# A gated linear-attention block and an MLP on one core: nine of twelve down products by Strassen's scheme

## The chip, the cores and the metric

The kernel runs on one core of one Trainium2 chip. The metric is device time in microseconds, from the start of the program to its end. Beside it one execution is recorded by the hardware profiler, and its page, its groups of instructions, its waits and its instructions in order of time are what this document reads. The engines are TensorE (PE in the profile, with its weight loads as PEld), VectorE (DVE), ScalarE (ACT), GpSimd (POOL) and SyncE (SP, which here only issues transfers). On-chip memory is SBUF; TensorE's results land in PSUM, which here is four pairs of banks.

## The reference

Two blocks follow one another. The first is a recurrence over 768 steps for 4 batches and 8 heads of 40 channels; the second is an MLP over the 3072 tokens that it yields, with 320 inputs, 2048 hidden units and 320 outputs.

```
for t in range(S):                                  # S = 768, state is 40x40 per batch and head
    y[:, :, t] = einsum('bhd,bhde->bhe', r_t, state)
    Sa = einsum('bhde,bhe->bhd', state, a_t)
    state = state * w_t - einsum('bhd,bhe->bhde', Sa, b_t) + einsum('bhd,bhe->bhde', v_t, k_t)
x = y.transpose(0, 2, 1, 3).reshape(3072, 320)
h = x @ w_in                                        # [3072, 2048]
g = h * (1.0 / (1.0 + exp(-1.702 * h)))
return g @ w_out                                    # [3072, 320]
```

All data are float32.

## The kernel before

The 768 steps are cut into twelve chunks of 64. A chunk has two units, each with two of the four batches, so there are 24 units `i = 2 * c + p`. For a unit, `decay` builds products of the decays, `prep` scales a, b and k by them and forms the score matrices, `inverse` inverts a triangular matrix in five levels, and `solve` reads the state, solves, and yields y and the next state. The level loop is a chain over engines: TensorE multiplies into `ps_level`, ScalarE or VectorE copies W out (line 751), VectorE forms E (line 753) and transposes it (line 702), and one of three engines spreads it into EX (lines 704 to 710), which the next level's product reads.

At its end a unit scales y into `x` (line 953) and writes it to DRAM (`part_with`, line 963); `get_back` (line 967) reads it back in the layout that the MLP wants, as `xT`. Both are issued on SP's queue. After a chunk's second unit `mlp(c)` follows for its 256 tokens:

- `up(q, m, k)`, line 978: the hidden layer, in four quarters q; eight matmuls of 256 columns in each of ten steps of a quarter.
- `gelu(q)`, line 987: ScalarE takes a quarter out of PSUM into a tile `g`, four of which exist.
- `down(p)`, line 992: the output of one half of the tokens (batches 2p and 2p + 1), in eight `part(m)` of 16 matmuls. The tokens are the stationary side (64x64), and 320 columns of `w_out_sb` stream past. One bank pair holds the sum over all of the hidden units, its two banks one half of the rows each. ScalarE or VectorE copies one bank to `ob` (line 1012), VectorE adds the other (line 1014), SP stores (line 1011).

A matmul of float32 appears as two instructions in the profile, and `mm` (line 299) is the line of them all. Four matmuls of 64x64 occupy the four quadrants of TensorE's array at once; the text calls four such instructions a pass.

The order of all work is written out by hand. `Plan.add` (line 65) records each piece as a task with the engines that could run it, its reads and writes; `listed` (line 89) reads the string `ORDER`, in which each entry names a task, its engine (p TensorE, a ScalarE, d VectorE, g GpSimd, s SyncE) and, where it uses PSUM, the bank pair. So an entry like `97g` puts task 97 on GpSimd at that place of its queue. The tasks of the MLP fill TensorE between the steps of the units' chains. The weights arrive as 64-bit numbers and are turned to float32 in the first stage (`weight`, line 431), with `extra` as one of the places for the raw numbers.

Of the kernel before, what the change touches and what calls it, by code (L numbers as in the profile page):

```python
# [58 lines left out]
class Plan:  # L59
# [29 lines left out]
    def listed(self, text):  # L89

        assert len(text.split()) == len(self.tasks)
        table, out, done = "exp", [], set()
        for one in text.split():
            e = next(e for e in ENGINES if ENGINES[e] in one)
            n, bank = one.split(ENGINES[e])
            t = self.tasks[int(n)]
            assert e in t.engines and t.after <= done and (e == "SP" or (t.pair is None) == (not bank))
            t.engine, t.bank = e, int(bank or 0)
            if e == "ACT" and t.table:
                t.load, table = t.table != table, t.table  # L100
            done.add(t)
            out.append(t)
        return out
# [4 lines left out]
0s 8s 26s 5s 7s 9s 3a 6s 87p0 88p1 24s 89a1 1s 2s 12s 102a 95d 100p2 90a0 93d 158a 101d2 98p3 96g 10s 94d 17s 97g 16s 99d3  # L108
103p1 4a 11s 132p0 104a1 105d1 142p2 143p3 133a0 106d 130p1 14s 144a3 13s 107p0 15s 18s 151g 108a0 109d0 51s 131a1 110p3 27s
149g 150d 111a3 112d3 159p0 156p1 145a2 161d0 160a0 152g 113p3 345s 92a 162d 25s 153d 114a3 163p2 42s 115d3 34s 19a 274s 264p0  # L110
165d2 265p3 164a2 22d 266a3 166p2 20d 273s 21d 33s 43s 167a2 154p3 168d2 23g 35s 28a 157d1 116p2 155d3 169p1 117a2 118d2 267a0
279d 63s 280g 119p3 277s 171d1 36s 44s 123a3 120d3 343s 125d3 121a 278g 124d3 29d 287a 126p2 170a1 288p0 127a2 30d 172p1 479s
122a3 31d 289a0 128p2 54s 173a1 45s 129d2 32g 62s 174d1 134p3 37a 290d0 175p2 344s 135d3 180a2 146s 178a2 275s 176d2 136p1
179a2 38d 181a2 39d 177a 282g 276s 291d 91s 138a1 182p0 188p3 281d 183a0 186p2 139d 137a1 283p0 187a2 184p1 189a3 40d 140s
292p2 46a 60s 284d0 41g 285p3 185d1 148a 286d3 190p0 293a2 294d2 334p1 335p3 357a 191d0 141s 268g 147s 336a3 315d 192p2 47d
337a1 348d 316p0 194a2 346s 295p3 349d 61s 317a0 195g 347s 358p1 296a3 297d3 360d1 318a0 298p3 271a 361d 319p0 338g 300d3 196s
193a2 320a0 355p2 385d 270s 48d 299a3 362p0 356d2 351g 301p3 363a0 364d0 350g 386p2 197s 302d3 365p0 387a2 269s 352g 359a1
303d3 388a2 323p1 367d0 366a0 321p3 49d 324a1 304p2 322a3 478s 325d1 50g 353p0 309a2 470p3 354d0 209p1 307a2 210p1 310a2 305d2
211p1 308a2 272d 198p0 341a 199p0 72s 212p1 70s 64a 200p0 340s 368p2 52s 342d 339s 69s 201p0 369a2 202p0 370d2 203p0 471a
213p1 65d 214p1 389p2 66d 472a3 483g 204p0 390a2 560s 371p3 67d 306a 53s 215p1 71s 482s 216p1 372a3 217p1 476a 220p2 373d3 68g  # L120
218p1 221p2 477d 219a1 205p0 222p2 206p0 223p2 224p2 78s 559s 207p0 55a 311p3 225p2 79s 312d3 80s 226p2 208a0 58d 313p1 374p3
314d1 227p2 56d 379a3 228p2 229p2 57d 326p0 230a2 59g 393p1 327d0 378a3 391p2 394a1 375d3 231p0 558s 392d2 376a 232p0 233p0
395d1 81s 73a 234p0 480s 381p2 235p0 474s 328p1 475s 382a2 74d 377a3 485d 380a3 236p0 75d 481s 492a 242p2 486d 243p2 82a 76d
484d 77g 383p3 237p0 384d3 244p2 329d1 330d1 488p3 473d 238p0 531d 245p2 487g 246p2 489d3 85d 532p1 708s 239p0 533a1 396p3
331d 534a1 240p0 247p2 397d3 332s 241a0 562s 535p1 83d 490p3 536a1 84d 398p0 706s 572a 491d3 86g 550p1 253p3 399d0 551a 555s
400d0 561s 333s 254p3 401d 255p3 552a1 564d 493p0 402s 556a 567g 570p1 554s 494d0 248p2 705s 563d 566g 249p2 495d0 498d 256p3
571d1 565g 403s 250a2 496a0 251d2 696p1 497g 557d 539p0 252s 537p2 257p3 538a2 704s 540d0 701s 258p3 553d 611d 697a 499d 573p2
259p3 576a2 574d2 784s 710d 700s 260p3 787s 541d0 575d2 404p0 578d 261a3 577g 405p0 579d 698a1 568p2 711g 500p1 406p0 569d2
501a1 407p0 262d3 580p2 702a 502d1 263s 408p0 582d2 409p0 503d 410p0 583d 504a 612p3 411p0 584g 613d3 412p0 614d3 413p0 505p1
709d 414a0 426p3 506d1 427p3 428p3 507d1 429p3 699d 581d2 430p3 615p1 703d 431p3 616a1 785s 585p0 432p3 508d 586a0 433p3 587d0  # L130
434p3 509a 588d 435p3 589d 448p2 436a3 510p1 590p0 511a1 449p2 592d0 591a0 512d1 415p3 513d 416p3 593d 514a 417p3 594g 418p3
515p0 419p3 516a0 517d0 595p1 518d 420p3 596a1 597d1 421p3 598d 422p3 519a 599d 423p3 424p3 520p0 425a3 437p1 521d0 438p1
523d0 522g 439p1 524d0 440p1 525d0 441p1 442p1 526d0 527p3 718p0 528a3 443p1 719d0 929s 444p1 720d0 529p3 445p1 721d0 446p1
530d3 600p0 723d 447a1 542p3 722d 724g 603d0 605a0 619p1 604d0 543d3 450p2 620a1 606d0 544p3 621d1 601d0 602d 617p1 707s 546d3
451p2 618a1 783s 712d 547g 713d 607p0 725p1 608a0 452p2 609p0 453p2 548s 610d0 932s 454p2 727d1 726d1 622p0 728d 545d3 729a
775p1 455p2 623d0 780s 776a 549s 756d 730p3 624p0 456d2 457d2 731d3 458s 459p2 777a1 778g 732d3 786s 788g 781a 779s 626d0
460p2 625d0 627g 733d 795p1 835d 734a 461p2 735p3 791g 462p2 628s 736a3 796d1 737d3 716p0 792g 738d 463p2 782d 739g 1011s
920p1 757p3 925s 464p2 717d0 758a3 629s 759a3 790d 465p2 740p0 789d 466p2 741a0 742d0 921a 797p3 467d2 760p0 1008s 468d2 800a3
923d 652p2 469s 761d0 922a1 653p2 926a 930s 798d3 714p1 799d3 654p2 924s 802d 801g 655p2 934d 803a 656p2 836p0 657p2 715d1
658p2 659p2 837d0 762p3 838d0 927d 660p2 763a3 661p2 764p1 662a2 743d 630p0 744d 928s 631p0 632p0 765d1 804p3 766d1 633p0  # L140
805a3 806d3 634p0 807d 635p0 808a 745p2 636p0 748d2 637p0 749d2 839p1 933g 750d2 638p0 840a1 1009s 751d2 639p0 809p3 746d2
935g 640a0 641p1 810d3 642p1 793p2 747a 811d3 674p0 812d 794d2 813a 752p3 643p1 753a3 814p2 644p1 815a2 816d2 754p3 645p1
755d3 646p1 817d 647p1 818a 767p2 841p3 768d2 648p1 842a3 649p1 819p2 650p1 820a2 821d2 769p3 822d 651a1 823d 675p0 771d3 931s
770d3 772g 824p2 936d 676p0 827a2 828a2 942p1 829a2 677p0 1153s 830a2 937d 945a1 773s 663p3 825d2 664p3 943d1 1156s 826a 665p3
944d1 999p2 947d 946g 666p3 1000a 1004s 980d 940p1 948g 667p3 941d1 668p3 774s 669p3 670p3 831p1 671p3 1001a2 1002d 1003s
832d1 672p3 1005a 1013d 678p0 673a3 1006d 833p2 843p1 679p0 834d2 1007s 844d1 938p2 845d1 680p0 939d2 846p3 681p0 847d3 949p1
1012g 682d0 848p2 950a1 683d0 1014d 684s 685p3 849d2 1015g 1010s 850d2 1021p0 1016g 951d1 686p3 1024a0 1232s 851d 1235s 981p2
687p3 982a2 952d 852s 1022d0 983a2 953g 1144p1 1023d0 688p3 1026d 1145a 1149s 1025d 1027g 984p2 1059d 689p3 1154s 954p0 853s
985a2 1147g 690p3 1158d 1148s 955a0 956d0 986p2 1146a1 957d 1150a 691p3 958d 987a2 1151d 988p0 692p3 989a0 1152s 990d0 959p1
693a3 865p2 960a1 694d3 866p2 961d1 867p2 695s 962d 868p2 963d 1028p0 869p2 1029a0 1030d0 870p2 1031d 1157g 871p2 1159d 1032a  # L150
1060p3 872p2 873p2 1061a3 874p2 1062d3 1033p1 875a2 854p0 1035d1 855p0 1036d 856p0 1037d 1063p3 857p0 1064d3 1034a1 858p0
964p2 859p0 965a2 966d2 1038p1 967d 860p0 1039a1 1040d1 861p0 1041d 1017p3 968a 1042g 862p0 1018d3 863p0 969p2 864a0 876p1
970d2 877p1 972d2 971g 1043p3 973d2 878p1 1044a3 974d2 879p1 975d2 880p1 881p1 1045d3 1019p0 1046d 976p2 1047a 882p1 1020d0
1233s 883p1 977a2 1166p3 884p1 1169a3 1167d3 1377s 978p0 885p1 1168d3 898p2 1171d 1170g 886a1 979d0 887p3 1172a 1048p0 991p1
1051a0 888p3 1052a0 992d1 889p3 1053a0 890p3 1054a0 891p3 1049d0 993p1 1050a 1067p0 994d1 1160g 1155s 892p3 1161d 1068a0 893p3
894p3 1069d0 1380s 895p3 1204d 1065p0 995d1 896p3 996d 1066a0 1231s 1055p1 899p2 897a3 1056d1 997s 1173p0 1223p3 900p2 1174a0
# [92 lines left out]
def rwkv7_gelu_quick(ctx: ExitStack, tc: tile.TileContext, time_d, v_d, w_d, wc_d, ak_d, b_d, rv_d, w_in, w_out, out):  # L249
    nc = tc.nc  # L250
    H, D, S = 8, 40, out.shape[0] // 4
    DM = H * D
    C = 64
    MID = C // 2
    NU = time_d.shape[0]
    PIECE = w_in.shape[2]
    NF = w_in.shape[0] * PIECE // DM
# [717 lines left out]
    def mlp(c):  # L975
# [47 lines left out]
        for p in BITS:  # L1023
            down(p)
# [8 lines left out]
    for i in range(NU):  # L1033
# [10 lines left out]
        if i % 2:  # L1044
            mlp(i // 2)
# [84 lines left out]
```

## Time and profile before

| | |
|---|---|
| median of 3 runs | 680.31 us (679.8 to 680.98) |
| profiled execution | 682.79 us, span 681.1 us |
| VectorE, ScalarE, GpSimd busy | 65%, 49%, 26% |
| mean granted TensorE clock | 0.990 of full speed |
| HBM traffic over the span | 98 GB/s |
| `ps_up` matmuls, 3840 of 256 columns | 254.4 us busy |
| `ps_down` matmuls, 3072 of 320 columns | 240.3 us busy |

A busy time is the union of the group's instructions, with pipelined and modelled ends, so the groups of TensorE overlap. The chain of waits gives `ps_up` 30.7% and `ps_down` 29.7% of the span, without overlap. The page's lines for one group name the line, engine and operation, out<-in with shapes and count, then busy time and the mean in ns, then the idle time of the engine just before, and what ended it.

### The profile page before, as it was taken

To read this page: it belongs to the slowest core of one execution; us is meant where nothing else is said; L and a number is where in the kernel's file an instruction comes from. 1 tells how busy PE (TensorE), PEld (TensorE's weight loads), DVE (VectorE), ACT (ScalarE), POOL (GpSimd) and SP (SyncE) were. 2 spreads that over 40 slices of the span, in tenths; PEclk is the share of its full clock that TensorE was granted. 3 is DMA by queue.
4 is the path that set the end of the run, shared out by engine and by line. 5 is a ranking of instruction groups with operands and counts; after the bars stand their busy time and mean duration, and the time that the engine had idled before them with its cause. 6 is when DMAs were issued, how large, how long until landed. Compare 5 with 4: busy or idle time off the path is not lost.

```text
span 681.1 us, 42181 instructions
## 1 busy us (share of the span) xinstructions
PE 652.0 (96%) x19488; PEld 572.4 (84%) x19488; DVE 445.5 (65%) x906; ACT 330.7 (49%) x688; POOL 176.7 (26%) x204
## 2 busy tenths in 40 slices
PE   5777999999999999999999999999999999999997
PEld 5667888997987788888888898899899799889996
DVE  4687877777867668767776587868556766675001
ACT  4675845544564654664545445455454354252110
POOL 5443444225123123123123211321412421300000
PEclk9788999999999999999999999999999999999999
DMA  7874755205314314432404413513502312200100
GB/s 235 275 244 148 228 158 173 89 14 155 108 50 139 103 45 125 124 108 67 121 23 131 140 34 107 154 33 106 149 29 71 121 51 58 58 13 23 51 12 21
DMA packets 35312, 69.73 MB, mean 102 GB/s; under 512 B 5440, under 2 KB 14656, under 8 KB 35136
## 3 DMA queue, kind: packets, MB, share of 16 engines
q1 hardware_dynamic: 35136, 67.03, 32.8%
q8 instruction: 153, 2.51, 1.6%
q14 instruction: 23, 0.19, 0.1%
HBM read 59.15 MB, written 7.86 MB: 98 GB/s over the span
## 4 chain that ended last, share of the span: by engine, by line
PE 91%; DMA 4%; ACT 1%; DVE 1%; issue 1%; SPq 0%; ACTq 0%; DVEq 0%
PE ps_up L300 31%; PE ps_down L300 30%; PE ps_level L300 9%; PE ps_y L300 5%; PE ps_B L300 4%; PE ps_X L300 2%; PE ps_N L300 2%; PE ps_rz L300 2%; PE ps_RV L300 2%; PE ps_A L300 1%; DMA ak<-in_ak 1%; PE ps_zT L300 1%; PE ps_Q L300 1%; DMA time<-in_time 1%; PE ps_T L300 1%
## 5 line engine op out<-in xcount | busy, mean ns | idle before, releaser
L300 PE MATMUL ps_up<-xT_all,w_sb 64*64 64x256 f32 x3840 | 254.4, 377 | 2.0 <-DMA xT_all<-x_dram 1.1
L300 PE MATMUL ps_down<-w_sb,g 64*64 64x320 f32 x3072 | 240.3, 430 | 1.1 <-issue 0.9
L300 PEld LDWEIGHTS ps_up<-xT_all,w_sb 64*64 64x64 f32 x3840 | 172.9, 133 | 17.7 <-issue 2.5
L300 PEld LDWEIGHTS ps_down<-w_sb,g 64*64 64x64 f32 x3072 | 143.3, 133 | 31.4 <-issue 1.6
L988 ACT ACTIVATE g<-ps_up 128x1024 f32<-128x1024 f32 x48 | 49.1, 1024 | 44.7 <-PE ps_up L300 44.3
L709 POOL TENSOR_TENSOR EX<-ES,quads 128x512 f32<-128x512 f32 x29 | 38.3, 1323 | 115.5 <-DVE ES L702 83.1
L751 ACT COPY W<-ps_level 128x512 f32<-128x512 f32 x56 | 32.7, 585 | 69.1 <-PE ps_level L300 67.4
L300 PEld LDWEIGHTS ps_level<-W,EX 64*64 64x64 f32 x2560 | 59.2, 134 | 5.8 <-DVE T L830 0.2
L300 PE MATMUL ps_level<-W,EX 64*64 64x64 f32 (+1 forms) x2560 | 56.2, 217 | 0.0
L753 DVE TENSOR_TENSOR E<-two,ps_level 128x256 f32<-128x256 f32 x80 | 33.1, 415 | 34.7 <-ACT W L751 30.7
L707 ACT ACTIVATE EX<-ES,quads 128x256 f32<-128x256 f32 x80 | 36.3, 501 | 30.4 <-DVE ES L702 29.9
L619 POOL TENSOR_TENSOR ak<-ak,FT 128x512 f32<-128x512 f32 x16 | 22.0, 1378 | 76.2 <-DMA ak<-in_ak 54.4
L300 PE MATMUL ps_level<-PT,EX 64*64 64x64 f32 (+2 forms) x1280 | 34.9, 244 | 5.7 <-DVE EX L723 4.8
L300 PEld LDWEIGHTS ps_level<-PT,EX 64*64 64x64 f32 x1280 | 32.6, 145 | 8.9 <-DVE EX L723 5.7
L702 DVE STREAM_TRANSPOSE ES<-E 128x256 f32<-128x256 f32 x80 | 35.2, 442 | 4.7 <-DVE E L753 0.5
L300 PE MATMUL ps_y<-M,bh 64*64 64x104 f32 (+1 forms) x768 | 34.8, 247 | 1.3 <-DVE M L907 0.8
L300 PE MATMUL ps_y<-RV,kh 64*64 64x104 f32 (+1 forms) x768 | 34.9, 247 | 0.3 <-DVE EX L723 0.3
L891 ACT COPY B<-ps_B 128x416 f32<-128x416 f32 (+1 forms) x34 | 16.5, 492 | 33.5 <-PE ps_B L300 33.2
L300 PEld LDWEIGHTS ps_y<-RV,kh 64*64 64x64 f32 x768 | 28.9, 133 | 2.0 <-DVE M L907 0.5
L907 DVE TENSOR_TENSOR M<-ps_X,later 128x832 f32<-128x832 f32 (+1 forms) x24 | 23.8, 993 | 9.8 <-PE ps_X L300 9.5
L627 POOL TENSOR_TENSOR kh<-time,G 128x320 f32<-128x320 f32 x18 | 16.2, 902 | 48.4 <-PE ps_y L300 34.4
L300 PEld LDWEIGHTS ps_y<-M,bh 64*64 64x64 f32 x768 | 27.0, 133 | 1.9 <-DVE M L907 1.2
(131 smaller groups left out, 1097.2 us busy)
## 6 DMA issues: line engine op xcount, KB each, us to landing
ak<-in_ak SPq DMA_DIRECT2D x48, 160.0 KB
rv<-in_rv SPq DMA_DIRECT2D x48, 160.0 KB
time<-in_time SPq DMA_DIRECT2D x24, 320.0 KB
xT_all<-x_dram SPq DMA_DIRECT2D x48, 160.0 KB
wc<-in_wc SPq DMA_DIRECT2D x20, 264.0 KB
logw<-in_w SPq DMA_DIRECT2D x24, 160.0 KB
RV<-in_v SPq DMA_DIRECT2D x24, 160.0 KB
b<-in_b SPq DMA_DIRECT2D x48, 80.0 KB
```

The costliest lines, as they stand in the source:

```text
L300: nc.tensor.matmul(o, lhsT, rhs, start=start, stop=True, skip_group_check=True)
L619: plan.add(R, {"DVE": 690.0, "POOL": 1270.0, "sbuf": True}, lambda t: of(t.engine).tensor_mul(ahT(), ahT(), FT_of(i)), reads=T("ak", "FT") ...
L627: plan.add(R + 4, {"POOL": 870.0, "DVE": 490.0, "sbuf": True}, lambda t, n=n, dst=dst: of(t.engine).tensor_mul(dst(i)[:, :, :D], by_head(t ...
L702: plan.add(rank, dve(256), lambda t: nc.vector.transpose(ES(n), source(t)), writes=[key("ES", n, 6)], **reads)
L707: nc.scalar.activation(dst[:, :, h], ES(n), ACT.Copy, scale=quads[:, h, :1])
L709: of(t.engine).tensor_mul(dst, ES(n).unsqueeze(2).to_broadcast([128, 8, 2, 32]), quads.unsqueeze(1).to_broadcast([128, 8, 2, 32]))
L751: plan.add(rank, any2(512), lambda t: copy(t.engine)(tiles_of(W(n + 1)), blocks(psum(t, ""), 64)), writes=[key("W", n + 1, 5)], pair=pair)
L753: plan.add(rank, dve(256), lambda t: nc.vector.tensor_sub(tiles_of(E(n + 1)), every(two32, [128, 2, 4, 32]), blocks(psum(t, ""), 64)[:, :, ...
L891: plan.add(R, any2(4 * wide), lambda t: copy(t.engine)(dst(), some(psum(t, "")[:, :, :208])), writes=[("Bv", i)] if x and c > 0 else T("B" ...
L907: plan.add(R + 1, dve(8 * wide), lambda t: nc.vector.tensor_tensor(M_of(i)[:, :, :wide].rearrange("p (j b) n -> p b j n", b=2), some(psum( ...
L988: plan.add(-45, {"ACT": 1030.0, "table": "gelu"}, lambda t: nc.scalar.activation(g_of(c * NQ + q).rearrange("p m r n -> p r m n"), psum(t, ...
```

## The change

For chunks 2 to 10 (`FAST`) the down product, a matrix of 256 tokens by 2048 hidden units times one of 2048 by 320, is cut into two halves along each of the three lengths and formed by seven block products in place of eight. `A11, A21, A12, A22` are blocks of g: the first index is the half of the tokens, the second which of two quarters of the hidden units (2j or 2j + 1). `B11` to `B22` are blocks of `w_out`, their second index the half of the columns. Chunks 0, 1 and 11 keep `down`.

- `factors`, once, before chunk 2's MLP: four combinations T1 to T4 of the weight blocks into `extra`, in eight subtractions of 640 elements a partition, on GpSimd or VectorE.
- `mixed`: for each chunk eight sums or differences of blocks of g, 512 elements a partition, on GpSimd or VectorE. S1 has a tile of its own; S2, S3 and S4 overwrite blocks of g once their products are formed.
- `product_of`: a block product in two steps (j), each of 32 matmul instructions of 160 columns. Three bank pairs take two, three and two products.
- `summed`: copies one bank out and adds the other, for 320, 480 and 320 elements; `added`: five small sums on GpSimd or VectorE. `store`: two tasks with two transfers each, from the new tile `of_fast`.
- The layout of g changes (blocks of 128 contiguous elements), with the reads of `gelu` and `down` that follow from it; g has six buffers in place of four; the scratch for GpSimd's own transfers is set to 2048 bytes.
- `ORDER` is another string, of 2825 entries in place of 2700. In it, by count, TensorE has 1062 tasks (1080), VectorE 814 (785), ScalarE 450 (433), GpSimd 231 (134) and SyncE 268 (268).

```diff
+    FAST = range(2, 11)
...
-                     A=1, B=1, RV=2, E0=2, W0=2, P21=2, PT=2, W=2, E=2, ES=2, EX=2, T=2, Tc=1, QT=1, zraw=2, zT=1, M=2, x=1, xT=3, g=4, ob=1), 4)
+                     A=1, B=1, RV=2, E0=2, W0=2, P21=2, PT=2, W=2, E=2, ES=2, EX=2, T=2, Tc=1, QT=1, zraw=2, zT=1, M=2, x=1, xT=3, g=6, ob=1, S10=1, S11=1, of=1, n6=1, n7=1), 4)
...
-    g_of = lambda n: buf("g", n, [128, 2, 2, 256])
+    g_of = lambda n: buf("g", n, [128, 2, 4, 128])
+    DH = DM // 2
+    S1 = single("S1", [128, 2, 4, 128])
+    T1, T2, T3, T4 = (extra[:, k * PIECE:(k + 1) * PIECE].rearrange("p (j f n) -> p j f n", j=2, f=4) for k in range(4))
+    B11, B12, B21, B22 = (w_out_sb.rearrange("p (j s f d n) -> p j s f d n", j=2, s=2, f=4, d=2)[:, :, s, :, d] for s in BITS for d in BITS)
+    of_fast, new6, new7 = (single(name, [128, n, DH]) for name, n in (("of_fast", 4), ("new6", 3), ("new7", 2)))
+
+    def light(n):
+        return {"POOL": 270.0 + 2.1 * n, "DVE": 165.0 + 1.03 * n, "sbuf": True}
+
+    def factors():
+        staged = [("weight", n) for n in range(len(raws))]
+        for dst, a, b, name, reads in ((T1, B12, B11, "T1", staged), (T2, B22, T1, "T2", [("T1", 0)]),
+                                       (T3, B22, B12, "T3", staged), (T4, B21, T2, "T4", [("T2", 0)])):
+            for j in BITS:
+                plan.add(10000, light(640), lambda t, dst=dst, a=a, b=b, j=j: of(t.engine).tensor_sub(dst[:, j], a[:, j], b[:, j]),
+                         reads=reads, writes=[(name, 0)])
+
+    def fast_down(c):
+        R = 10000 + 100 * c
+        A11, A21, A12, A22 = (lambda j, s=s, p=p: g_of(c * NQ + 2 * j + s)[:, p] for s in BITS for p in BITS)
+        g = lambda j, *which: [("g", c * NQ + 2 * j + s) for s in which]
+        T = lambda *names: [(name, c) for name in names]
+        s1 = lambda j: S1[:, j]
+
+        def mixed(j, name, dst, a, b, reads, writes, add=False):
+            def go(t):
+                (of(t.engine).tensor_add if add else of(t.engine).tensor_sub)(dst(j), a(j), b(j))
+            plan.add(-44, light(512), go, reads=reads, writes=writes + [(f"{name}{j}", c)])
+
+        def product_of(pair, n, at, a, b, j, reads):
+            def go(t):
+                po = psum(t, "ps_fast")
+                for f in range(4):
+                    for r, h in QUARTERS:
+                        mm(po[HALF[h], r, at * DH:(at + 1) * DH], a(j)[HALF[r], 2 * (f % 2) + f // 2, h * 64:h * 64 + 64], b[HALF[r], j, f], at == 0 and j == 0 and f == 0)
+            plan.add(R + 20 + n, pe((4, DH)), go, reads=reads, writes=T(f"M{n}{j}"), pair=("down", (c, pair)), most=1)
+
+        def summed(pair, n, dst, key, name):
+            flat = lambda: dst().rearrange("p k n -> p (k n)")
+            plan.add(-45, any2(n * DH), lambda t: copy(t.engine)(flat(), psum(t, "")[:, 0, :n * DH]), writes=T(key), pair=("down", (c, pair)))
+            plan.add(-45, dve(n * DH), lambda t: nc.vector.tensor_add(flat(), flat(), psum(t, "")[:, 1, :n * DH]),
+                     reads=T(key), writes=T(name), pair=("down", (c, pair)))
+
+        def added(dst, a, b, n, reads, uses, name):
+            plan.add(-45, light(n * DH), lambda t: of(t.engine).tensor_add(dst(), a(), b()), reads=T(*reads), uses=T(*uses), writes=T(name))
...
+        for j in BITS:
+            mixed(j, "A", s1, A21, A22, g(j, 0, 1), T(f"S1{j}"), add=True)
+            mixed(j, "S3", A21, A11, A21, g(j, 0) + T(f"A{j}"), [])
+        for j in BITS:
+            product_of(0, 2, 0, A12, B21, j, g(j, 1) + [("weight", NQ + 2 * j + 1)])
+            product_of(0, 1, 1, A11, B11, j, g(j, 0) + [("weight", NQ + 2 * j)])
+        for j in BITS:
+            mixed(j, "S2", A11, s1, A11, g(j, 0) + T(f"S1{j}", f"S3{j}", f"M1{j}"), [])
+            mixed(j, "S4", A12, A12, A11, g(j, 0, 1) + T(f"S2{j}", f"M2{j}"), [])
+        summed(0, 2, lambda: of_fast[:, :2], "of", "M21")
+        added(lambda: of_fast[:, 0], lambda: of_fast[:, 0], lambda: of_fast[:, 1], 1, ["M21"], ["of"], "C11")
+        for j in BITS:
+            product_of(1, 4, 0, A22, T4, j, g(j, 1) + [("T4", 0)])
+        for j in BITS:
+            product_of(1, 5, 1, s1, T1, j, T(f"S1{j}") + [("T1", 0)])
+        for j in BITS:
+            product_of(1, 6, 2, A11, T2, j, g(j, 0) + T(f"S2{j}") + [("T2", 0)])
+        summed(1, 3, lambda: new6, "n6", "M456")
...
+        for j in BITS:
+            product_of(2, 7, 0, A21, T3, j, g(j, 0) + T(f"S3{j}") + [("T3", 0)])
+            product_of(2, 3, 1, A12, B22, j, g(j, 1) + T(f"S4{j}") + [("weight", NQ + 2 * j + 1)])
+        summed(2, 2, lambda: new7, "n7", "M73")
...
+        store(0, ["C11", "C12"])
+        store(1, ["C2"])
...
-        for p in BITS:
-            down(p)
+        if c in FAST:
+            fast_down(c)
+        else:
+            for p in BITS:
+                down(p)
```

The sums left out in the cut are the five of `added`: C11, U, XW, C12 and C2, of 160, 160, 320, 160 and 320 elements.

## The prediction

> **What bounds the kernel.** I read the page first, then busy time by stage, then the instructions in order of time around the products and around the last handover.
>
> ```profile
> span 681.1 us, 42181 instructions
> ...
> PE 652.0 (96%) x19488; PEld 572.4 (84%) x19488; DVE 445.5 (65%) x906; ACT 330.7 (49%) x688; POOL 176.7 (26%) x204
> ...
> PE ps_up L300 31%; PE ps_down L300 30%; PE ps_level L300 9%; PE ps_y L300 5%; PE ps_B L300 4%; PE ps_X L300 2%; PE ps_N L300 2%; PE ps_rz L300 2%; PE ps_RV L300 2%; PE ps_A L300 1%; DMA ak<-in_ak 1%; PE ps_zT L300 1%; PE ps_Q L300 1%; DMA time<-in_time 1%; PE ps_T L300 1%
> ```
>
> ```profile
> core 0: us, PE busy (x) PEld busy (x) DVE busy (x) ACT busy (x) POOL busy (x), PEclk, DMA share, GB/s
> ...
> 142.00:199.00 57.00, 56.33 (x1794) 48.05 (x1790) 41.64 (x93) 27.74 (x56) 14.46 (x18) 1.00 0.30 89
> 199.00:256.00 57.00, 57.00 (x1776) 45.11 (x1771) 40.06 (x83) 32.75 (x71) 16.31 (x17) 1.00 0.33 97
> 256.00:313.00 57.00, 57.00 (x1756) 47.79 (x1747) 41.75 (x86) 34.06 (x65) 15.93 (x16) 1.00 0.39 114
> ```
>
> TensorE is the path, and the down product is 30% of it. From 199 to 484 us TensorE is never idle; from 85 to 640 us its windows lack 3.4 us (1.40, 0.67, 1.30 and 0.05). The other idle time, some 20 us, lies in the first 85 us. There the order of TensorE's work is unchanged: its first 170 tasks are the same in both order strings. So whatever TensorE is spared after that is won, unless a new wait takes it back.
>
> **The removal and the addition on TensorE.** What does a stream of 160 columns cost against one of 320?
>
> ```profile
> 325.21 0.67 PE L300 MATMUL ps_level<-W,EX 64*64 64x64 f32 x32
> 325.67 2.36 PE L300 MATMUL ps_down<-w_sb,g 64*64 64x320 f32 x32
> 327.83 0.67 PE L300 MATMUL ps_level<-PT,EX 64*64 64x64 f32 x32
> 328.29 0.48 PE L300 MATMUL ps_cum<-logw,edges 64*64 64x160 f32 x8
> 328.56 1.28 PE L300 MATMUL ps_down<-w_sb,g 64*64 64x320 f32 x16
> 329.64 0.56 PE L300 MATMUL ps_B<-RV,A 64*64 64x104 f32 x16
> ```
>
> Start to start: a `part` of `down` (16 matmuls of 320 columns) takes 1.08 us; eight matmuls of 160 columns take 0.27 us. Four quadrants run at once, so these are four and two passes, at 270 and 135 ns. Long runs fix the decimals: in the chain of waits 208 down matmuls take 14.02 us, 269.6 ns a pass (1.078 us a part), and the 64 of `ps_y` with 104 columns 1.43 us, 89.4 ns. The straight line through these two gives 136.1 ns at 160 columns. A `product_of` is 32 matmuls, eight passes, 1.089 us. A chunk had 16 parts, 17.25 us, and gets 14 products, 15.24 us: 2.01 us less, **18.1 us over nine chunks**. With 135 and 137.5 ns a pass, the ends that the 160-column rows allow (0.27 to 0.275 for two), it is 19.2 and 16.6.
>
> The loads double per column: nine chunks have 448 weight loads each in place of 256. I cost them at nothing, since 32 matmuls of 64 columns with 32 loads take 0.46 us (325.21 to 325.67), 58 ns a pass; four loads fit under 58 ns and so under 135.
>
> [...]
>
> **The sums around the products.** A fast chunk adds 8 mixes of 512 elements, 3 copies and 3 adds from PSUM (320, 480, 320), and 5 small sums; it drops 2 copies and 2 adds of 320. Durations:
>
> ```profile
> L709 POOL TENSOR_TENSOR EX<-ES,quads 128x512 f32<-128x512 f32 x29 | 38.3, 1323 | 115.5 <-DVE ES L702 83.1
> ...
> L627 POOL TENSOR_TENSOR kh<-time,G 128x320 f32<-128x320 f32 x18 | 16.2, 902 | 48.4 <-PE ps_y L300 34.4
> ```
>
> On DVE the same 512 elements take 0.70 us, a 320 copy 0.49, a 320 add 0.48; ACT copies 320 in 0.43. I counted who runs what in the two order strings: GpSimd goes from 134 tasks to 231, VectorE 785 to 814, ScalarE 433 to 450. With row durations (160 and 480 elements and the 640 of the factors between and beyond neighbours) GpSimd gains 104 us (83 new, 21 taken over from VectorE), VectorE 18, ScalarE 10 and two more table changes. Per fast chunk that is +11.5, +2.0 and +1.1 us against the means of the five windows 199 to 484 (15.1, 41.4, 29.8 of 57): about 48%, 79% and 56% of a 55 us chunk. None becomes the bound. The cover is TensorE's other work, 40 `up` sets and two units; where it is missing a mix costs its whole 0.7 or 1.3 us. In the order the inputs of the 126 products end at least 0.3 us of TensorE work ahead of them; one falls short by 0.1.
>
> **Waits.** Three terms.
> (1) Unit chains. For every TensorE task after the first 60 us I summed the TensorE work listed between its last input's start and itself, less that input's row duration. Under 0.3 us remain for 60 of 511 tasks before and 71 of 493 after; the shortfalls below zero sum to 8.6 and 14.2 us. 8.6 showed as 3.4 of idle, so 5.6 more should show as 2.2. Bounds: 0 and 5.6.
> (2) GpSimd and VectorE in each other's way.
>
> ```profile
> L845 DVE TENSOR_TENSOR zr<-zraw,wz x22: 443/488/1566, 52.4 to 585.8; 128x320 f32<-128x320 f32 x22
> ```
>
> That row (least, median, most) has a mean of 593 beside a median of 488; at 291.1 us a GpSimd mix took 1.79 rather than 1.28 while VectorE multiplied two SBUF tiles. The excess over the least in four such groups (`zr`, `ak` on both engines) is some 10 us. With 1.6 times the GpSimd work 6 to 12 us more fall on engines with 11 us of slack a chunk, about 1 us a chunk; I put 0.5 us in all on the path, bounds 0 and 12.
> [...]
> (3) Handovers. `up` of a chunk waits for x to go to DRAM and back. The last one before:
>
> ```profile
> 628.86 0.69 DVE L943 TENSOR_TENSOR zr<-ps_y,zr 128x512 f32<-128x512 f32 x1 [2.39 <-PE ps_y L300]
> 629.58 0.90 DVE L953 TENSOR_TENSOR x<-zr,FT 128x128 f32<-128x128 f32 x4
> 630.51 0.66 SPq L963 DMA_DIRECT2D x_dram<-x  x2
> ...
> 634.13 1.13 SPq L1011 DMA_DIRECT2D out<-ob  x2
> 635.36 1.19 SPq L967 DMA_DIRECT2D xT_all<-x_dram  x2
> 638.99 4.45 PEld L300 LDWEIGHTS ps_up<-xT_all,w_sb 64*64 64x64 f32 x80
> ```
>
> The new order lists eight products (8.7 us) there in place of ten parts (10.8). The trip takes 1.9 us from the end of `ps_y` to the issue, 2.2 to 3.1 to the second (as at 573.47 and 625.88), at most 3.6 to landing: 7.7 to 8.6, as no store stands ahead in SP's queue now. At chunk 2 the cover goes from 12.0 to 9.2 us, and the trip took 11.5 (162.1 to about 173.6). I take 0.3 and 1.0 us, bounds 0 and 1.9, 0 and 2.3. Chunk 8, where `ps_up` waited 1.1 us, loses 0.4 us of cover; elsewhere it is equal or longer.
> The tail keeps its form: last part, copy, add, store. Stores stay 48 transfers; `of_fast` has one buffer, so the next chunk's first copy waits for this chunk's stores; they stand 6.9 us or more of TensorE work ahead.
>
> **The sum.** 18.1 less 2.2, 0.5 and 1.3 is 14.1 us. The span of 681.1 becomes 667.0, the profiled time of 682.79 (1.7 around the span) 668.7. The median of the runs, 680.31, lies 2.5 lower than the profiled one: **666 us** forecast.
>
> **Rivals.**
> - All waits stay covered: 680.3 - 18.1, **662 us**. For it: no idle from 199 to 484. Against: covers shrink in the order. 0.13.
> - Half the gain goes: terms 1 to 3 near their upper ends but for contention (5.6, 2 and 4.2, 12 us): **674 us**. 0.15.
> - Slower: the level chains of the units run late. Nine chunks have 90 level steps, each a transpose and a spread before the next `ps_level`, and a VectorE at 79% with GpSimd holding it up can delay each. From 18.1/90 = 0.20 us a step on TensorE the gain is gone; at 0.3 us it is **689 us**. For it: 4.8 us of `ps_level` waiting for EX already, the 1566 ns. Against: over 285 us no step reached TensorE. 0.09, of it 0.02 within the band.
> - Weight loads show, so that it is no saving: a pass of 136 + 58 ns makes 14 products 21.7 us, 4.5 more a chunk: **721 us**. Against: the 160-column row, loads included. 0.03.
>
> The forecast's own case (662 to 670) has 0.60. The range 660 to 676 leaves out the last two and a third of the second, under 2 in 10. A change of 0.2% is about what a measurement of this kernel can tell from none: faster 0.13 + 0.15 + 0.60 = 0.88, within 0.02, slower 0.10.
>
> **What would show it.** TensorE's matmuls go from 19488 to 21216 (+192 a chunk), its busy time from 652 to about 634; 32 matmuls of 160 columns start to start in 1.08 to 1.10 us; GpSimd near 280 us, VectorE 465 to 480; idle after 85 us at 6 to 8 us, some of it before chunk 2's and 11's first `ps_up`. I am wrong if the products take over 1.12 us, or if TensorE waits for EX, T or M by more than 10 us.

## The result, and the profile after

Forecast 666 us, measured 709.19 us (median of 4 runs, 706.37 to 712.94) against 680.05 us (4 runs). The ratio is 1.043, with a 95% interval of 1.0373 to 1.0487. The kernel became 29 us slower where 14 less were forecast. The profiled execution has a span of 709.1 us beside 681.1, at a mean granted clock of 0.987 beside 0.990. A run over 1.5% above the fastest of its kernel, as one of four of `split` below, is left out of medians and ratios.

Of the page before, the instruction queue and the chain of waits:

```profile
q8 instruction: 153, 2.51, 1.6%
...
PE 91%; DMA 4%; ACT 1%; DVE 1%; issue 1%; SPq 0%; ACTq 0%; DVEq 0%
```

The page after the change, its busy times, its instruction queue, its chain of waits and two groups:

```profile
span 709.1 us, 45708 instructions
...
PE 655.7 (92%) x21216; PEld 590.7 (83%) x21216; DVE 474.6 (67%) x909; ACT 340.1 (48%) x724; POOL 275.9 (39%) x307
...
q8 instruction: 167, 2.74, 1.6%
...
PE 85%; DVE 6%; issue 4%; DMA 3%; ACT 1%; SPq 0%; DVEq 0%; ACTq 0%
...
L309 PE MATMUL ps_fast<-extra,g 64*64 64x160 f32 x1728 | 74.9, 297 | 2.7 <-issue 2.6
L309 PE MATMUL ps_fast<-w_sb,g 64*64 64x160 f32 x1728 | 72.9, 297 | 1.8 <-issue 1.8
```

VectorE (474.6) and GpSimd (275.9) came out as forecast, and so did the 21216 matmuls. TensorE did not lose 18 us of busy time but gained 4. "issue" is 4% of the chain, some 28 us, where it was 1%; it is time in which the engine waited for nothing that the profile shows. The middle stages, with 0.67, 0 and 0 us of idle time before, have more now:

```profile
core 0: us, PE busy (x) PEld busy (x) DVE busy (x) ACT busy (x) POOL busy (x), PEclk, DMA share, GB/s
142.00:199.00 57.00, 54.93 (x1751) 44.78 (x1743) 45.67 (x85) 29.28 (x69) 20.97 (x22) 1.00 0.29 86
199.00:256.00 57.00, 54.62 (x1902) 50.19 (x1897) 42.41 (x87) 29.58 (x62) 26.05 (x27) 1.00 0.31 92
256.00:313.00 57.00, 53.23 (x1800) 48.48 (x1796) 37.84 (x77) 30.88 (x62) 24.17 (x25) 1.00 0.30 90
```

From 199 to 313 us 6.15 us are idle, at full clock. TensorE's idle time by what ended it (line, what was waited for, us in total, times, longest):

```profile
PE ps_level L309 <- issue: 7.7, 10, 1.6
PE ps_fast L309 <- issue: 4.4, 8, 0.7
...
PE ps_level L309 <- DVE EX L732: 2.8, 4, 1.3
...
PE ps_up L309 <- DMA xT_all<-x_dram: 1.1, 2, 0.6
```

The waits that the prediction feared, for EX and for `x`, are small; the largest one names no other engine. Where it falls is seen in the order of time (start, us, what; in brackets the idle time before):

```profile
330.18 0.36 PE L309 MATMUL ps_y<-RV,kh 64*64 64x104 f32 x8
330.35 0.25 PE L309 MATMUL ps_y<-M,bh 64*64 64x104 f32 x1
332.13 0.32 PE L309 MATMUL ps_y<-M,bh 64*64 64x104 f32 x4 [1.52 <-issue]
...
335.92 1.05 PE L309 MATMUL ps_fast<-w_sb,g 64*64 64x160 f32 x24 [0.49 <-issue]
...
339.73 0.35 PE L309 MATMUL ps_cum<-logw,edges 64*64 64x160 f32 x1 [0.48 <-issue]
```

The first stall lies between the first and the next of eight matmuls with the same inputs and the same output bank: nothing that a task could wait for changes there. The three stalls come 3.8 us apart. Queue 8 of the page brings instructions: 167 transfers, 2.74 MB in all, 16.4 KB each. The trace has 42703 instructions of TensorE, which makes 64 bytes an instruction and 256 a transfer; before the change it was 39272 instructions and 153 transfers. Set beside the trace's records of that queue:

```
stall ends    block had landed    us after    matmuls and loads since the stall before
332.13        330.74              1.39
335.92        334.70              1.22        254
339.73        338.49              1.24        253
```

So each stall ends 1.2 to 1.4 us after a block of instructions lands, and with those of TensorE's sequencer (waits and the like) there are exactly 256 instructions from one stall to the next, both times. I counted all gaps over 250 ns between starts of TensorE's instructions after the first 80 us, each less 40 ns. Those that end 1.07 to 1.73 us after a block: 7 with 4.2 us in all before the change, 48 with **32.2 us** after it. All others: 2.9 and 7.7 us. Numbered through, sequencer's included, 46 of the 48 stalls (31.0 us) stand before the same place of every 256 instructions, and none of the others does; so do 5 of the 7 before the change. A wait for another engine would fall there by chance alone.

A full account follows from TensorE's time, from its first start to its last, less an ideal stream (0.833 ns a column and 2.7 ns a pass, and 58 ns at least: in the trace of before the median pass takes 269.25 ns at 320 columns, 89.25 at 104 and 58.25 at 64). That ideal is 632.7 us before and 614.6 after, 18.1 less, as forecast. The time beyond it grew from 33.4 to 36.9 us in the first 85 us and from 6.0 to 48.5 behind them. 3.5 and 42.5 less 18.1 are the 28.0 us between the spans. The 42.5 are 28.0 of block gaps, 4.8 of other gaps, and 9.7 that are left for gaps under 250 ns.

### The profile page after: what moved, and what is told of

The parts are those of the page before. It is cut to its first block, busy times and chain, and to the rows that moved or that the text cites. A ratio compares the mean times of both kernels' runs of the same rounds, so it can differ in the third digit from the quotient of the medians.

```text
span 709.1 us, 45708 instructions
## 1 busy us (share of the span) xinstructions
PE 655.7 (92%) x21216; PEld 590.7 (83%) x21216; DVE 474.6 (67%) x909; ACT 340.1 (48%) x724; POOL 275.9 (39%) x307
## 3 DMA queue, kind: packets, MB, share of 16 engines
q8 instruction: 167, 2.74, 1.6%
## 4 chain that ended last, share of the span: by engine, by line
PE 85%; DVE 6%; issue 4%; DMA 3%; ACT 1%; SPq 0%; DVEq 0%; ACTq 0%
PE ps_up L309 28%; PE ps_fast L309 18%; PE ps_level L309 10%; PE ps_down L309 7%; PE ps_B L309 5%; PE ps_y L309 5%; PE ps_X L309 2%; PE ps_RV L309 2%; PE ps_rz L309 2%; PE ps_N L309 2%; PE ps_A L309 1%; DMA xT_all<-x_dram 1%; PE ps_zT L309 1%; PE ps_Q L309 1%; DMA rv<-in_rv 1%
## 5 line engine op out<-in xcount | busy, mean ns | idle before, releaser
L309 PE MATMUL ps_fast<-extra,g 64*64 64x160 f32 x1728 | 74.9, 297 | 2.7 <-issue 2.6
L309 PE MATMUL ps_fast<-w_sb,g 64*64 64x160 f32 x1728 | 72.9, 297 | 1.8 <-issue 1.8
L309 PEld LDWEIGHTS ps_fast<-extra,g 64*64 64x64 f32 x1728 | 62.6, 133 | 5.1 <-issue 4.5
L309 PEld LDWEIGHTS ps_fast<-w_sb,g 64*64 64x64 f32 x1728 | 61.9, 133 | 3.3 <-issue 2.9
L716 ACT ACTIVATE EX<-ES,quads 128x256 f32<-128x256 f32 x92 | 41.5, 502 | 43.3 <-DVE ES L711 43.3
L718 POOL TENSOR_TENSOR EX<-ES,quads 128x512 f32<-128x512 f32 x25 | 33.2, 1330 | 65.6 <-DVE ES L711 62.6
L309 PE MATMUL ps_down<-w_sb,g 64*64 64x320 f32 x768 | 58.1, 430 | 0.0
L309 PEld LDWEIGHTS ps_down<-w_sb,g 64*64 64x64 f32 x768 | 34.8, 133 | 11.4
L806 ACT COPY Tc<-ps_level 32x64 f32<-32x64 f32 x128 | 25.8, 202 | 38.0 <-DVE ES L711 15.0
L309 PEld LDWEIGHTS ps_level<-PT,EX 64*64 64x64 f32 x1280 | 33.4, 147 | 9.0 <-issue 2.8
L1011 POOL TENSOR_TENSOR g<-g 128x512 f32<-128x512 f32 x22 | 30.6, 1390 | 19.5 <-DVE S L1011 11.8
```

Of the source, the lines that this page charges most:

```text
L309: nc.tensor.matmul(o, lhsT, rhs, start=start, stop=True, skip_group_check=True)
L716: nc.scalar.activation(dst[:, :, h], ES(n), ACT.Copy, scale=quads[:, h, :1])
L718: of(t.engine).tensor_mul(dst, ES(n).unsqueeze(2).to_broadcast([128, 8, 2, 32]), quads.unsqueeze(1).to_broadcast([128, 8, 2, 32]))
L806: copy(t.engine)(dst, src[:, u, :, f])
L1011: (of(t.engine).tensor_add if add else of(t.engine).tensor_sub)(dst(j), a(j), b(j))
```

## The experiments

The theory from here on is that TensorE's **instruction supply** holds it: where a stretch of work uses instructions faster than blocks come, it runs dry. The rivals: (a) a 160-column stream with its loads is slow in itself; (b) the new order or late VectorE and GpSimd work stalls TensorE, and "issue" is only how this shows. Each experiment was timed beside the kernel before, 678.6 to 681.5 us there.

**1. More instructions without the change (split).** The kernel before, its order, engines and sums; in chunks 2 to 10 every down matmul of 320 columns is issued as two of 160.

```diff
-                            mm(po[HALF[b], r, :DM], g[HALF[r], f % 2, o:o + 64], w_out_sb[HALF[r], f * DM:(f + 1) * DM], f == 0)
+                            if not 2 <= c <= 10:
+                                mm(po[HALF[b], r, :DM], g[HALF[r], f % 2, o:o + 64], w_out_sb[HALF[r], f * DM:(f + 1) * DM], f == 0)
+                        if 2 <= c <= 10:
+                            for n in BITS:
+                                for r, b in QUARTERS:
+                                    o = p * 128 + b * 64
+                                    mm(po[HALF[b], r, n * 160:(n + 1) * 160], g[HALF[r], f % 2, o:o + 64],
+                                       w_out_sb[HALF[r], f * DM + n * 160:f * DM + (n + 1) * 160], f == 0 and n == 0)
```

> The kernel before with its own order; in chunks 2 to 10 each down matmul of 320 columns is issued as two of 160, so TensorE has 43584 matmuls and weight loads in place of 38976 (the changed kernel: 42432) and the same columns to stream. If TensorE is held up by the supply of its instructions: slower, 705 to 730 us, with idle TensorE inside runs of matmuls that wait for nothing. If the new order and the late vector work cost the time: 680 to 684, since neither is in it. If a matmul of 160 columns is slow by itself (the 47 us that the changed kernel lost against the forecast's 18 us gain, over 1008 passes, are 47 ns a pass): 1152 such passes, about 735.

Measured: 716.77 us, ratio 1.056 [1.0489, 1.0632], as the supply expects. Its page:

```profile
span 710.1 us, 46789 instructions
...
PE 662.1 (93%) x21792; PEld 613.5 (86%) x21792; DVE 445.4 (63%) x906; ACT 330.6 (47%) x688; POOL 175.4 (25%) x204
...
L300 PE MATMUL ps_down<-w_sb,g 64*64 64x160 f32 (+1 forms) x5376 | 256.2, 316 | 12.3 <-issue 11.9
```

VectorE and GpSimd do what they did before the change, and no sum and no order is new; yet 38 us are lost against the 678.6 beside it, with the same "issue" waits and 31.6 us of block gaps. The order and the vector work (b) are not needed for the loss.

**2. Fewer instructions with the change (fewer), and fewer still (fewest).** The changed kernel, where the products issue only two, or only one, of the four quadrants' matmuls from the second of the four steps on. The passes stay: where the one quadrant of fewest works alone, its matmuls start 136 ns apart, as a pass of four does.

```diff
-                    for r, h in QUARTERS:
+                    for r, h in QUARTERS if f == 0 else QUARTERS[:2]:
```

> The changed kernel with its own order; three of four f steps of a product use two of the four quadrants, so that part of the down product of nine chunks is left out. Columns per quadrant and vector work stay, TensorE's matmuls and loads fall from 42432 to 39408 (before: 38976). Supply of instructions: 664 to 684 us. Order and late vector work: 703 to 710, as nothing of them is touched. Slow 160-column matmuls: about 690, as fewer loads stand beside each stream.

> As the run fewer, with one quadrant in place of two in three of four f steps (more of the down product of nine chunks is left out): 37896 matmuls and loads, under the 38976 of before, with the order, the columns and the vector work of the changed kernel. Supply of instructions: of the 14 us of gaps at a block's end that the run fewer has left, half or more go: 672 to 680 us. If what the run fewer has left are waits of the order: 682 to 686, unchanged.

Measured: fewer 684.44 us, 1.0091 [1.0057, 1.0126]; fewest 678.29 us, 0.9992 [0.9964, 1.0019]. The page of fewer:

```profile
span 681.4 us, 42684 instructions
...
PE 639.1 (94%) x19704; PEld 581.1 (85%) x19704; DVE 471.3 (69%) x909; ACT 339.9 (50%) x724; POOL 276.0 (40%) x307
...
L309 PE MATMUL ps_fast<-extra,g 64*64 64x160 f32 x1080 | 72.9, 299 | 0.1
L309 PE MATMUL ps_fast<-w_sb,g 64*64 64x160 f32 x1080 | 71.7, 298 | 0.4 <-issue 0.4
```

The products occupy TensorE as long as with all of their instructions (72.9 and 71.7 us beside 74.9 and 72.9), all other engines work as before, and 25 us are gone; with 1512 instructions less again, 31, and the products' two rows still have 72.0 and 70.1 us. Block gaps are 14.2 and 8.6 us. Time follows the number of TensorE's instructions:

```
kernel    ideal stream, us    matmuls and loads    block gaps, us    median, us
split     as before           43584                31.6              716.8
after     18 less             42432                32.2              709.2
fewer     18 less             39408                14.2              684.4
before    as before           38976                 4.2              680.1
fewest    18 less             37896                 8.6              678.3
```

The ideal stream is that of the account above; in the third and the last row it is counted by passes. Fewest came out as the supply expects, and fewer 0.4 us above its range; order and late vector work, which both kernels keep, had 703 to 710 for fewer. Fewest lies 12 us above the forecast: what then remains is the subject of runs 6 and 7.

**3. The supply by itself (supply, supply_dma).** A kernel that computes nothing of the reference: long runs of quadrant matmuls on zeros, 768 passes a width, then the output is stored. The second has SP load 160 KB tiles beside it, two under way at a time.

```diff
+    bufs_ = [const.tile([128, 320], FP32, tag=f"in{i}", name=f"in{i}") for i in range(2)]
+    for i in range(300):
+        nc.sync.dma_start(bufs_[i % 2], src.rearrange("(n p) d -> n p d", p=128)[i % 24])
```

> Only a stream of quadrant matmuls on zeros (the output is zeros, all of the computation is left out), with no transfers beside it until the end: 768 passes each of 160, 64, 104 and again 160 columns, 6144 matmuls and loads a stage, with short stages of 256 columns between. Supply of instructions, at one block of 256 in about 3.9 us as the changed kernel's trace shows where TensorE starves: the stages of 64 and 104 columns take about 95 us each in place of 45 and 69, those of 160 columns 104 us (59 instructions per us, under the supply). Slow 160-column matmuls: 140 us for each stage of 160. Order: says nothing of it.

> The run supply with 300 loads of 160 KB issued beside it on the queue of SP, two under way at a time (again only a stream on zeros, all of the computation is left out). If transfers of data slow the blocks of instructions: the 64-column stage, while loads run, takes 92 to 100 us in place of 84.6 (a block in 3.9 us or more in place of 3.5). If they do not: 84 to 86.

Measured in one run of each, from the first to the last start of 768 passes: 160 columns 104.2 us (135.85 ns a pass), without and with the loads. 64 columns 84.6 us where the stream alone would be 44.5, and 91.6 with the loads; 104 columns 85.7 where it would be 69, and 92.9. Two widths that take the same time are not limited by columns. 160 columns with loads of their own are not slow (rival a). The order of time in the stage of 64 columns, without the loads:

```profile
172.12 2.09 PE L38 MATMUL ps<-x,w 64*64 64x64 f32 x128 [1.36 <-issue]
175.57 2.09 PE L38 MATMUL ps<-x,w 64*64 64x64 f32 x128 [1.36 <-issue]
```

128 matmuls, with their loads 256 instructions, run in 2.09 us, 58 ns from pass to pass, and then TensorE waits 1.36 us for the next block: 3.45 us a block. After the first 80 us all 45 stalls of this run stand before the same place of every 256 instructions. With the loads it is like this:

```profile
170.28 2.09 PE L41 MATMUL ps<-x,w 64*64 64x64 f32 x128 [1.64 <-issue]
174.56 3.06 PE L41 MATMUL ps<-x,w 64*64 64x64 f32 x128 [2.19 <-issue]
178.28 2.29 PE L41 MATMUL ps<-x,w 64*64 64x64 f32 x128 [0.66 <-issue]
```

Over the stage that is 72.6 instructions per us (8 a pass, 6144 in 84.6 us) and, beside transfers of 108 GB/s, 67.1, a block per 3.82 us, which is the distance of the stalls at 330 to 340 us above. The quiet run supplied more than its expectation had taken from the stalls (84.6 us, not 95), and the loads slow it about as much as expected. They are not the only difference: in the stage of 64 columns the granted clock fell to 0.92 with the loads. In that of 104 columns it was 1.00 in both runs, and the slowing is the same.

**4. Products with fewer, larger matmuls (wide, tall).** If the number of instructions is what costs, larger tiles should cure it. wide: the four quadrants' matmuls of a step as one on the whole array; tall: as two, of 64 rows by 128 columns. The first diff is that of wide, the second that of tall.

```diff
-                    for r, h in QUARTERS:
-                        mm(po[HALF[h], r, at * DH:(at + 1) * DH], a(j)[HALF[r], 2 * (f % 2) + f // 2, h * 64:h * 64 + 64], b[HALF[r], j, f], at == 0 and j == 0 and f == 0)
+                    mm(po[:, f % 2, at * DH:(at + 1) * DH], a(j)[:, 2 * (f % 2) + f // 2, :128], b[:, j, f], at == 0 and j == 0 and f < 2)
```

```diff
-                    for r, h in QUARTERS:
-                        mm(po[HALF[h], r, at * DH:(at + 1) * DH], a(j)[HALF[r], 2 * (f % 2) + f // 2, h * 64:h * 64 + 64], b[HALF[r], j, f], at == 0 and j == 0 and f == 0)
+                    for r in BITS:
+                        mm(po[:, r, at * DH:(at + 1) * DH], a(j)[HALF[r], 2 * (f % 2) + f // 2, :128], b[HALF[r], j, f], at == 0 and j == 0 and f == 0)
```

> The changed kernel with its own order; a product uses the whole array (128 rows by 128 columns) in one matmul in place of four quadrants, alternate f steps in the two banks, so the result and all of the vector work stay. TensorE's matmuls and loads fall from 42432 to 36384. Supply of instructions: 655 to 672 us, unless a change between whole-array and quadrant matmuls costs time itself. Order and late vector work: 703 to 710. Slow 160-column matmuls: between, 685 to 700.

> The changed kernel and its order; a product uses two matmuls of 64 rows by 128 columns a step in place of four quadrants: same columns, same two banks, same sums, TensorE's matmuls and loads 38400 in place of 42432. Supply of instructions: 668 to 684 us. If a change from quadrants to another shape costs about 0.2 us a product, as it did for the whole array: about 700. If only the order and late vector work were left to explain the time: 703 to 710.

Measured: wide 703.12 us, 1.0346 [1.0285, 1.0407]; tall 705.97 us, 1.0361 [1.0317, 1.0405]. Both miss the gain that the supply alone would bring, and lie at the 700 to 710 us of the other two cases. Block gaps did fall, to 8.6 and 11.6 us, but another cost took their place. The products of wide in order of time:

```profile
305.25 1.35 PE L309 MATMUL ps_fast<-w_sb,g 128*128 128x160 f32 x8
306.53 0.50 PE L309 MATMUL ps_cum<-logw,edges 64*64 64x160 f32 x8
...
314.09 1.35 PE L309 MATMUL ps_fast<-w_sb,g 128*128 128x160 f32 x8
315.38 0.69 PE L309 MATMUL ps_A<-ak 40*64 40x64 f32 x32
```

From start to start a product takes 1.28 and 1.29 us where quadrants took 1.09, though within the eight matmuls the starts are the same 136 ns apart. The 126 products of wide stand in 84 stretches, 55 of them of one product, at a median of 1.28 us, 23 of two, at 2.37, and the longest of eight, 8.89 us: it is 0.2 us a stretch over 1.09 a product, some 17 us in all. Two more kernels test whether the change of shape is what costs: all of the MLP in 64 by 128 tiles, in the changed kernel (tall_all) and in the kernel before (tall_before), which then have few instructions (33792 and 32064) and many changes of shape. `up` is edited as shown, and `down` in the same way.

```diff
-                for r, h in QUARTERS:
-                    mm(ph[HALF[h], r, m * 256:(m + 1) * 256], w_in_sb[HALF[r], 2 * q + m, k, h * 64:(h + 1) * 64], x[HALF[r]],
-                       m == 0 and k == 0)
+                for r in BITS:
+                    mm(ph[:, r, m * 256:(m + 1) * 256], w_in_sb[HALF[r], 2 * q + m, k], x[HALF[r]], m == 0 and k == 0)
```

> As the run tall, and up and down in the same shape too: 33792 matmuls and loads, and fewer changes of shape, since up and the products stand side by side. Supply of instructions: the forecast's gain comes back less the other waits (4.8 us beside the blocks and 3.6 us in the first 85 us by the trace of the changed kernel): 680 - 18.1 + 8.4, 668 to 674 us. If a change of shape costs time: 690 or more. Order and late vector work: 703 to 710.

> The kernel before and its order, with up and down in the shape of 64 rows by 128 columns: 32064 matmuls and loads in place of 38976. Supply of instructions: 674 to 680 us, since only 4.2 us of the kernel before are gaps at a block's end. If a change of shape costs time: 690 or more.

Measured: 744.15 us, 1.0953 [1.093, 1.0977], and 774.96 us, 1.1406 [1.1382, 1.143]: the change of shape costs. The kernel before, with tall tiles:

```profile
310.16 0.69 PE L300 MATMUL ps_RV<-rv 40*64 40x64 f32 x32
310.78 1.35 PE L300 MATMUL ps_down<-w_sb,g 64*128 64x320 f32 x8
312.06 0.69 PE L300 MATMUL ps_level<-W,EX 64*64 64x64 f32 x32
312.68 1.35 PE L300 MATMUL ps_down<-w_sb,g 64*128 64x320 f32 x8
```

A part takes 1.28 us in place of 1.08, and a level product 0.62 in place of 0.46: each change costs on both sides. The second kernel has the old order and the old vector work, so neither makes the larger tiles slow. Larger tiles were no cure in these four kernels, where the units' small products lie between them.

**5. The change where little else runs (late).** The kernel before, with Strassen's scheme in chunks 10 and 11 alone and the order around them rewritten by hand.

```diff
+    FAST = (10, 11)
...
+        if c in FAST:
+            fast_down(c)
...
```

> The kernel before with its own order up to the end of its last unit, and the seven products of the changed kernel for chunks 10 and 11 alone, whose products lie at the end, where few unit tasks are left and up and down ask for 30 to 37 instructions a us of TensorE. Supply of instructions: the four products saved are kept, 4 x 1.08 us, less some 0.6 us of sums after the last product: 676.5 us where before has 680 (ratio 0.994 to 0.996). If a product of 160 columns costs more than a part by itself, or the sums hold up the end: no gain or a loss, 680 to 690.

Measured: 680.32 us over 12 runs, 1.0009 [0.9985, 1.0032]: no gain that can be told, and not the 676.5 us that the supply expected. It lies where the expectation put its rivals, of which a slow product is ruled out by run 3; whether the sums hold up the end stays open. The profiled execution (span 674.3) is the lowest of the twelve. There the last stalls behind a block end at 623.1 and 627.5 us (0.9 and 0.4 us between starts), with none in the last 46 us; why the median shows nothing of the products saved, this run does not tell.

**6. Less vector work with all of TensorE's instructions (idle_vec).** Six of the eight mixes of a chunk work on 32 of 512 elements, so that rival (b) is tested alone.

```diff
-                (of(t.engine).tensor_add if add else of(t.engine).tensor_sub)(dst(j), a(j), b(j))
+                n = 4 if add else 1
+                (of(t.engine).tensor_add if add else of(t.engine).tensor_sub)(dst(j)[:, :n, :128 if add else 32], a(j)[:, :n, :128 if add else 32], b(j)[:, :n, :128 if add else 32])
```

> The changed kernel, its order and all of its TensorE instructions; six of the eight mixes of a chunk (S2, S3, S4) work on 32 of their 512 elements, so that most of these three sums are left out and GpSimd and VectorE have some 40 us and 10 us less to do. Supply of instructions: 702 to 709 us, TensorE's instructions being the same. [...]

Measured: 715.71 us, 1.0487 [1.042, 1.0555], above the 702 to 709 us that the supply expects, with an interval that overlaps that of the whole change. VectorE's busy time fell to 454.4 us and GpSimd's to 242.5, and nothing is won: block gaps are 39.2 us, 57 of the 58 at the same place of every 256 instructions. TensorE's largest waits there:

```profile
PE ps_level L309 <- issue: 7.2, 10, 1.5
PE ps_fast L309 <- issue: 5.9, 12, 1.1
```

**7. Both together (fewest_idle).** The edits of fewest and of idle_vec in one kernel.

> The run fewest with the same six mixes cut to 32 of 512 elements, so that parts of the products and of these sums are left out. If what the run fewest still loses against the forecast (678 against 666) is vector work that comes late: 668 to 673 us. If it is the rest of the block gaps or the order itself: 675 to 680.

Measured: 678.84 us, 0.9975 [0.9941, 1.0008], as fewest. The 12 us between fewest and the forecast are not late vector work either. By the records of fewest, block gaps are still 8.6 us (4.2 before), other gaps 9.1 (2.9): 10.6 us more than before, where the forecast had 4.0 for all waits. That is 6.6 us of the 7.5 by which its profiled span, 674.5 us, misses the forecast one of 667.0. The other 4.3 of the 12 lie between profiled runs and medians: the forecast took off the 2.5 us by which the profiled run of before stands above its median, while that of fewest stands 1.8 below. How much of the other gaps is the order's, no run separates.

## Why the prediction was wrong, point by point

- **The saving on TensorE**, 18.1 us: the size is right. A pass of 160 columns takes 135.85 ns in a run of 768, and where a product's 32 matmuls stand together in the trace of after, the median from start to start is 1.09 us (41 of 44 within 1.13). The two signs of being wrong did not appear: the median product stays under 1.12 us, and the waits of TensorE for EX, T and M came to 8.5 us in all, under the 10. Both signs watched streams and producers, and what failed was neither.
- **The loads**: "The loads double per column: nine chunks have 448 weight loads each in place of 256. I cost them at nothing, since ..." **This is the step that failed.** The evidence for it, 32 matmuls of 64 columns with their loads at 58 ns a pass, is a burst of 64 instructions, a quarter of a block. The supply run has 256 of them at that speed and then a wait, so a short burst tells nothing of the rate at which instructions come. 58 ns a pass use 138 instructions per us; the supply run shows 72.6 and, with traffic, 67.1. The change raised TensorE's demand after 85 us from 59 to 67 matmuls and loads per us of ideal stream (34744 in 584.8 us, 38434 in 570.4). A chunk gains 384 instructions, one and a half blocks. With a mean so near the supply's rate, I take it, only a reserve could even out `up` (37 per us), products (59) and unit steps (90 to 138, at 104 and 64 columns). The records show little of one: the start of a transfer stands at a nearly fixed place of the work, within 254 instructions, less than a block, before the change and 220 after it. Taking instructions away gave 31 of the 43 us missed.
- **Unit chains**, 2.2 us, and **handovers**, 1.3 us: their sum is about right, though no run splits it. Gaps that end at no block grew by 4.8 us after 80 us, with 4.0 forecast for all three terms. The chain of waits around chunk 2's handover, forecast at 1.0 us, which left TensorE 0.8 us between two instructions:

```profile
167.67 4.05 DVE x L962 x4
...
172.08 1.77 DMA x_dram<-x
...
175.88 3.20 DMA xT_all<-x_dram
...
179.12 0.88 PE ps_up L309 x12
```

- **VectorE and GpSimd in each other's way**, 0.5 us on the path: the first of these lines fits it, four scalings of `x` in 4.05 us where the last handover before had 0.90; GpSimd worked beside them without a pause from 167.81 to 171.56 us, on one of the `factors` among others. What it costs on the path in all, no run gives; with most of the mixes cut in idle_vec, nothing was won.
- **TensorE's busy time**, forecast at 634 us, was 656. The ends of its instructions are modelled, so where instructions come slowly, but with gaps shorter than their duration, the row counts it as busy: of 1.77 us between starts at 332.13, the waits show 1.52.
- **The rivals.** "Weight loads show", 721 us at 0.03, had the sign and the nearest number, and the wrong mechanism: a pass is not 58 ns longer, and 14 products at 1.087 us (eight passes of 135.85 ns) are 15.2 us, not 21.7. The level chains (689 us) fall with idle_vec, and with the waits themselves: `ps_level` waited 2.8 us for EX on VectorE, 4.8 before.

What could have been read beforehand: the page's 153 transfers on queue 8, one per 4.45 us of the span, and two stalls of the kernel before, which end at 90.26 and 95.95 us, 1.46 and 1.41 us after blocks that landed at 88.80 and 94.54. There the supply was already a block per 5.7 us, beside 211 GB/s of transfers (window of 83 to 96 us):

```profile
90.26 0.87 PE L300 MATMUL ps_up<-xT_all,w_sb 64*64 64x256 f32 x11 [0.48 <-issue]
...
95.95 1.03 PE L300 MATMUL ps_down<-w_sb,g 64*64 64x320 f32 x12 [0.92 <-issue]
```

## What to carry to other kernels

Count instructions as well as time: an engine with many short instructions has a demand per us of its work, and a scheme that saves arithmetic by cutting work into smaller pieces raises it, here from 59 to 67 matmuls and loads per us. Take the supply from the distance of the instruction queue's transfers where the engine stalls without a releaser in the middle of a task, and look at it over at least two blocks, never from a short burst: 64 instructions here ran at 58 ns a pass, 138 per us, while blocks brought 72.6. A stall that keeps its place in every block of instructions, whatever the task, is the sign to look for (46 of 48 here). Larger tiles did not cure it here (703.12 and 705.97 us), as their neighbours had another shape.

## What the runs showed of the hardware

- TensorE's instructions come in blocks of 256: the page of after has 167 transfers of 16.4 KB on queue 8 for 42703 instructions, that of before 153 for 39272. In the stage of 64 columns a block comes per 3.53 us on average in the quiet run (supply) and per 3.82 us beside 108 GB/s of loads (supply_dma). After the change a block comes every 4.08 us on average after 85 us, before it every 4.27. The stalls at one place of every 256 instructions come to 31.0 us in the trace of after.
- A change between 64x64 quadrants and a larger tile costs about 0.2 us a piece: 1.28 us in place of 1.09 for a product of wide, 1.28 in place of 1.08 for a part of tall_before. What TensorE does in that time, no run shows.
- One quadrant alone takes as long as four at once, at 160 columns: in fewest, where one works alone, its matmuls start 136 ns apart, as passes of four do (135.85 ns in supply). The products of fewest, with one quadrant in three of four steps, have 72.0 and 70.1 us in their two rows beside 74.9 and 72.9 with four.
